# A new column order for the DFT table, and mirror rows stored block by block with plain transfers

## The chip, the cores and the metric

The kernel runs on one core of one Trainium2 chip. The metric is the device time of one execution in microseconds (us). A core has five engines that work side by side, each with an instruction stream of its own: TensorE (PE, with its weight loads shown as PEld), VectorE (DVE), ScalarE (ACT), GpSimd (POOL) and SyncE (SP). SP, ACT and POOL also issue the DMAs; 16 DMA engines carry them.

## The reference

For each of 8 sequences of 3072 tokens with 256 features, the real part of a two-dimensional discrete Fourier transform is taken, and a feed-forward layer with a three-way maximum works on every token:

```
X = np.fft.fft(np.fft.fft(x, axis=1), axis=2).real      # x: (8, 3072, 256)
t = X.reshape(8 * 3072, 256)
h = np.maximum(np.maximum(t @ w1, t @ w2), t @ w3)      # each w: (256, 768)
out = h @ w_out                                         # (768, 256), out: (24576, 256), fp32
```

Inputs and output are fp32. The real input makes token k and its mirror token 3072 - k of a sequence share their work: one is a sum, the other a difference of an even part and an odd part.

## The kernel before

**Stages.** A sequence is first mixed. x is loaded (line 127, POOL's queue, with a cast to bf16) into `xt`; short products with a small table give `tb` (lines 401 to 416); `tb` goes to DRAM as `db` and comes back transposed as `yb` (methods `y` and `z`, lines 419 to 431, SP's queue); then `Mix.k` (line 461) multiplies the 17 column groups of `yb` with the cosine tables `te_tab` and `to_tab`. That gives `tE` and `tO`, the even and the odd part, for 1536 half-tokens of the sequence, in three blocks of 512 columns. The cosine tables are made on the chip from a vector `kvec` of token numbers, by iotas (`ramp`, line 169), a reduction of the angle and sines.

**Column order.** Which token stands in which of the 1536 columns follows from which `yb` group the column is multiplied with. Before, the groups of 96 columns (64 for the last) follow one another: group r holds the tokens r, r + 32, r + 64 and so on. `_parts(g)` (line 39) lists for block g which group covers which columns; each entry is one matmul of `Mix.k` (line 466). A block has 6, 6 and 8 entries.

**The feed-forward layer.** Each block of 512 columns passes six units of 128 hidden features (`begin`, `finish`): `unit_plus` adds even and odd (`hp`, for the tokens), `unit_minus` turns the same sum into the difference (`hm`, for the mirror tokens). For every second unit (`is_split`) the third operand is summed outside PE: DVE makes `even3`, ACT `odd3`, and POOL their sum and difference, `plus` and `minus` (line 828), which DVE's `hp` (line 837) and `hm` (line 849) then need.

**The second layer** (`l2_block`, line 517) runs one block behind, as a generator from which ten steps are taken per unit. A block has four sub-blocks of 128 columns; a slot is a sub-block's number in its sequence, 0 to 11. PE gathers the token half and the mirror half in `po` (line 513), and DVE adds the linear part and writes `ot`, 128 x 512 fp32 (line 541), of which six buffers turn. Then

- the token half goes out on SP's queue in two or three plain stores (line 549). `_runs(slot)` (line 30) lists runs of partitions whose tokens are 32 rows apart in `out`; a row is 1 KB;
- the mirror half goes out on POOL's queue in one indexed store (line 622), emitted by `scatter` at the next unit. Its row numbers stand in `rows_m`, which `rows` (line 697) works out on POOL during the first sequence. Slot 11 stores 127 rows, since its first column is token 0. A one-element memset on `mark` (line 626) follows each.

The last block of the last sequence (`l2_last`, line 552) takes its sub-blocks in the order 3, 0, 1, 2, has the mirror half computed from flipped copies `tEr` and `tOr`, so that its rows ascend too, and issues plain stores from ACT, SP and POOL in turn (line 584). `l2_mid` (line 587) handles token 1536 of all sequences.

**Order.** The order on every engine is written out by hand: `plan` and `ahead` say at which unit of a sequence which piece of the next one's mixing is issued (the yb loads `z0` and `z1` at units 6 and 7), and each engine and queue runs its instructions in that order. DMAs of ACT and SP share eight completion counters in rotation, POOL's another eight.

Of the kernel before, what the change touches and what calls it, by code (L numbers as in the profile page):

```python
# [9 lines left out]
FP32 = mybir.dt.float32  # L10
BF16 = mybir.dt.bfloat16
INT32 = mybir.dt.int32
UINT32 = mybir.dt.uint32
AX = mybir.ActivationFunctionType
ALU = mybir.AluOpType
# [14 lines left out]
def _runs(slot):  # L30

    if slot == 11:
        return [(0, 48, 0), (48, 96, 16), (96, 128, 15 + 32 * 64)]
    t, u = divmod(slot, 3)
    edge, r = 96 - 32 * u, 4 * t + 1 + u
    return [(0, edge, r + 32 * 32 * u), (edge, 128, r + 1)]


def _parts(g):

    cols = [(r, 96 * (r - 1), 96 if r < 15 else 64, 0) for r in range(1, 16)]
    cols += [(0, 1408, 48, 0), (16, 1456, 48, 0), (15, 1504, 32, 64)]
    done = []
    for (r, c, wd, _) in cols:
        a, z = max(c, 512 * g), min(c + wd, 512 * g + 512)
        if a < z:
            done.append(((r - 1) % 16 if r < 16 else 16, a - 512 * g, z - a))
    return done
# [3 lines left out]
def kernel(  # L52
# [9 lines left out]
    nc = tc.nc  # L62

    B, S, D = x.shape
# [50 lines left out]
    rows_m = consts.tile([128, 12 * B], INT32, tag="rows_m")  # L115
    mark = consts.tile([1, 1], FP32, tag="mark")
# [32 lines left out]
    def iota(t, pattern, base=0, cm=0):  # L149
        nc.gpsimd.iota(t, pattern, base=base, channel_multiplier=cm,  # L150
                       allow_small_or_imprecise_dtypes=True)
# [14 lines left out]
    kvec = gen.tile([128, NHALF + 1], FP32, tag="kvec")  # L166
    kv = kvec[:, 0:1440].rearrange("p (r j) -> p r j", j=96)

    def ramp(r):
        n = {0: 6, 6: 5, 11: 4}[r]  # L170
        iota(kv[:, r:r + n, :], [[1, n], [32, 96]], base=r + 1)

    dvec = gen.tile([128, 128], FP32, tag="dvec")
    for c, (s0, s1) in enumerate(FIRST):
        for h in range(2):
            load_x(0, s0, s1, h)
        if c == 0:
            iota(dvec, [[1, 128]])
        elif c < 3:
            ramp((0, 6)[c - 1])  # L180
# [12 lines left out]
    ramp(11)  # L193
    iota(kvec[:, 1408:1504].rearrange("p (r j) -> p r j", r=2), [[16, 2], [32, 48]])
    iota(kvec[:, 1504:NHALF], [[32, 32]], base=15 + 32 * 64)
    iota(kvec[:, NHALF:NHALF + 1], [[0, 1]], base=NHALF)
# [72 lines left out]
    q = gen.tile([128, NHALF + 1], FP32, tag="q")  # L269
# [118 lines left out]
    class Mix:  # L388
# [72 lines left out]
        def k(self, which, g, evict=nc.scalar.copy):  # L461
# [3 lines left out]
            for (i, c0, wd) in _parts(g):  # L465
                nc.tensor.matmul(ps2[:, c0:c0 + wd], self.col(i, which),  # L466
                                 tab[:, g * 512 + c0:g * 512 + c0 + wd], start=True, stop=True)
# [38 lines left out]
    def stored(st, mine, others):  # L506
        for group in others:
            tc.declare_no_dep(st.ins, group=group, reason="each store has rows of its own")
        tc.add_to_no_dep_group(mine, st.ins)
# [7 lines left out]
    def l2_block(b, blk, hp, hm, te, to):  # L517

        base = b * S
        for sub in range(4):  # L520
# [3 lines left out]
            if sub % 2 == 0:  # L524
# [10 lines left out]
            ot = out_pool.tile([128, 512], FP32, name="ot", tag="ot")  # L535
# [6 lines left out]
                out=ot.rearrange("p (h c) -> p h c", h=2),  # L542
                in0=po.rearrange("p (h c) -> p h c", h=2),
                in1=lin.unsqueeze(1).to_broadcast([128, 2, 256]), op=ALU.add)
            lo = 1 if slot == 11 else 0
            waiting.append((b * 12 + slot, lo, ot))
            for (p0, p1, k0) in _runs(slot):
                row = base + k0
                stored(nc.sync.dma_start(out=out[row: row + 32 * (p1 - p0 - 1) + 1: 32, :],
                                         in_=ot[p0:p1, 0:256]), "direct", ("scattered",))  # L550

    def l2_last(hp, hm, te, to, flipped):

        base = (B - 1) * S
        ter, tor = flipped
        for sub in (3, 0, 1, 2):
# [4 lines left out]
            ot = out_pool.tile([128, 512], FP32, name="ot", tag="ot")  # L561
            for (h, tev, tov, wo, hid) in (
                    (0, te[:, cp], to[:, cp], gw[:, 256:512], lambda jc: hp[:, jc, sp]),
                    (1, ter[:, sm], tor[:, sm], gw[:, 512:768], lambda jc: hm[:, jc, sm])):
                if h == 0 or sub == 2:
                    po = ps_o.tile([128, 512], FP32, name="po", tag="po")
# [6 lines left out]
                if sub == 2:  # L573
                    nc.vector.tensor_copy(out=ot[:, h * 256:(h + 1) * 256], in_=ph)
            if sub != 2:
                nc.vector.tensor_copy(out=ot, in_=po)
            stores = [(p0, p1, base + k0, 0) for (p0, p1, k0) in _runs(slot)]
            for (p0, p1, k0) in _runs(slot):
                if k0 == 0:
                    p0, k0 = 1, 32  # L580
                stores.append((128 - p1, 128 - p0, base + S - k0 - 32 * (p1 - p0 - 1), 256))
            for k, (p0, p1, row, c) in enumerate(stores):
                eng = (nc.scalar, nc.sync, nc.gpsimd)[(k + (sub == 2)) % 3]
                stored(eng.dma_start(out=out[row: row + 32 * (p1 - p0 - 1) + 1: 32, :],
                                     in_=ot[p0:p1, c:c + 256]), "direct", ("scattered",))

    def l2_mid():
# [20 lines left out]
        for _ in l2_hidden(po[0:B, 0:256], lambda jc: hmid[:, jc, :]):  # L608
            pass
        ot = out_pool.tile([128, 512], FP32, name="ot", tag="ot")  # L610
        nc.vector.tensor_copy(out=ot[0:B, 0:256], in_=po[0:B, 0:256])
        stored(nc.sync.dma_start(out=out[NHALF: NHALF + S * (B - 1) + 1: S, :],
                                 in_=ot[0:B, 0:256]), "direct", ("scattered",))
# [4 lines left out]
    def scatter():  # L618

        while waiting:  # L620
            at_row, lo, ot = waiting.pop(0)
            stored(nc.gpsimd.indirect_dma_start(  # L622
                out, bass.IndirectOffsetOnAxis(
                    ap=rows_m[0:128 - lo, at_row: at_row + 1], axis=0),
                ot[lo:128, 256:512], None), "scattered", ("scattered", "direct"))
            nc.gpsimd.memset(mark, 0.0)
# [60 lines left out]
    m.c(1, 7)  # L687
# [9 lines left out]
    def rows():  # L697

        rows_f = gen.tile([128, 12 * B], FP32, tag="rows_f")
        iota(rows_f.rearrange("p (b t u) -> p b t u", t=4, u=3), [[S, B], [-4, 4], [-1025, 3]],  # L700
             base=S - 1, cm=-32)
        rows_v = rows_f.rearrange("p (b r) -> p b r", r=12)
        adj = gen.tile([128, 12], FP32, tag="adj")
        adv = adj.rearrange("p (t u) -> p t u", u=3)
        four = pidx.to_broadcast([128, 4])
        pool = nc.gpsimd
        for u in range(3):
            scal(adv[:, :, u], four, float(96 - 32 * u), ALU.is_ge, 3071.0, ALU.mult, eng=pool)
        low = gen.tile([128, 2], FP32, tag="low")
        scal(low[:, 0:1], pidx, 47.0, ALU.is_ge, 1520.0, ALU.mult, eng=pool)  # L710
        scal(low[:, 1:2], pidx, 95.0, ALU.is_ge, -511.0, ALU.mult, eng=pool)
        scal(low[:, 0:1], low[:, 0:1], 2031.0, ALU.add, eng=pool)
        pool.tensor_tensor(out=adj[:, 11:12], in0=low[:, 0:1], in1=low[:, 1:2], op=ALU.add)
        pool.tensor_tensor(out=rows_v, in0=rows_v,
                           in1=adj.unsqueeze(1).to_broadcast([128, B, 12]), op=ALU.add)
        pool.tensor_copy(rows_m, rows_f)

# [5 lines left out]
    out_pool = ctx.enter_context(tc.tile_pool(name="outbuf", bufs=6))  # L723
# [201 lines left out]
```

## Time and profile before

| | us |
|---|---|
| median of 3 runs (394.51 to 395.22) | 394.9 |
| the profiled execution | 395.75 |
| its span, first to last instruction | 393.8 |
| PE busy | 377.7 |
| POOL busy | 332.9 |
| DVE busy | 315.0 |
| ACT busy | 263.0 |

The span lies inside the profiled execution; the difference is what lies around the program's own instructions. Busy time is the time in which an engine has an instruction at work. The granted PE clock was 0.996 of full speed over the span. DMA moved 54.20 MB, 138 GB/s in the mean. A matmul's own duration includes its way through the array, so the pace of a stream of matmuls is read from start to start.

### The profile page before, as it was taken

To read this page: it belongs to the slowest core of one execution; us is meant where nothing else is said; L and a number is where in the kernel's file an instruction comes from. 1 tells how busy PE (TensorE), PEld (TensorE's weight loads), DVE (VectorE), ACT (ScalarE), POOL (GpSimd) and SP (SyncE) were. 2 spreads that over 40 slices of the span, in tenths; PEclk is the share of its full clock that TensorE was granted. 3 is DMA by queue.
4 is the path that set the end of the run, shared out by engine and by line. 5 is a ranking of instruction groups with operands and counts; after the bars stand their busy time and mean duration, and the time that the engine had idled before them with its cause. 6 is when DMAs were issued, how large, how long until landed. Compare 5 with 4: busy or idle time off the path is not lost.

```text
span 393.8 us, 8383 instructions
## 1 busy us (share of the span) xinstructions
PE 377.7 (96%) x2710; PEld 235.9 (60%) x2759; DVE 315.0 (80%) x530; ACT 263.0 (67%) x476; POOL 332.9 (85%) x432
## 2 busy tenths in 40 slices
PE   6698999999999999999999999999999999999994
PEld 2354566566665666565665666556665666666673
DVE  7788897788687788788787888877887887887972
ACT  6877788677766887577867787578866447435420
POOL 8985698979978899889988899889977898869993
PEclk9999999999999999999999999999999999999998
DMA  7999576585838776495767876495333553321234
GB/s 115 159 194 183 131 191 146 114 191 150 161 102 144 190 153 144 117 206 137 137 150 120 210 132 160 118 206 124 108 108 101 131 147 90 94 77 47 90 96 131
DMA packets 66901, 54.20 MB, mean 138 GB/s; under 512 B 32702, under 2 KB 62556, under 8 KB 66003
## 3 DMA queue, kind: packets, MB, share of 16 engines
q0 software_dynamic: 24368, 26.53, 35.5%
q1 hardware_dynamic: 41978, 26.72, 27.0%
q8 instruction: 21, 0.34, 0.4%
q10 hardware_dynamic: 512, 0.43, 0.4%
q14 instruction: 22, 0.18, 0.1%
HBM read 36.95 MB, written 30.81 MB: 172 GB/s over the span
## 4 chain that ended last, share of the span: by engine, by line
PE 84%; DMA 4%; DVE 4%; ACT 3%; issue 2%; POOL 2%; SPq 1%; DVEq 0%; ACTq 0%; POOLq 0%
PE po L513 30%; PE pse L497 12%; PE pse L490 8%; PE pse L491 7%; PE po L536 4%; PE d L821 4%; PE pse L835 4%; PE e L819 3%; PE ps L466 3%; PE pse L836 3%; PE pl L528 2%; PE ps L401 2%; DMA yb<-db 2%; DMA xt<-in_x_dram 2%; ACT tb L405 1%
## 5 line engine op out<-in xcount | busy, mean ns | idle before, releaser
L503 ACT ACTIVATE stmp<-pse 128x512 bf16<-128x512 f32 x150 | 89.6, 600 | 66.1 <-PE pse L497 50.9
L622 POOL DMA_INDIRECT out_dram<-ot,rows_m x92 | 102.4, 1113 | 17.9 <-issue 8.8
L828 POOL TENSOR_TENSOR plus<-even,odd 128x512 bf16<-128x512 f32 x69 | 87.8, 1272 | 32.9 <-DVE even L824 32.7
L828 POOL TENSOR_TENSOR minus<-even,odd 128x512 bf16<-128x512 f32 x69 | 87.5, 1268 | 0.0
L513 PE MATMUL po<-wout_bf,hp 128*128 128x256 bf16 x576 | 86.1, 273 | 0.4
L837 DVE SCALAR_TENSOR_TENSOR hp<-pse,plus 128x512 bf16<-128x512 f32 x69 | 47.6, 689 | 46.5 <-PE pse L836 13.9
L513 PE MATMUL po<-wout_bf,hm 128*128 128x256 bf16 x576 | 78.6, 273 | 0.0
L513 PEld LDWEIGHTS <-hp 128*128 128x128 bf16 x576 | 56.4, 98 | 26.1
L497 PE MATMUL pse<-tO,gd_all 128*128 128x512 bf16 x217 | 70.5, 379 | 1.1 <-DVE hp L504 0.2
L513 PEld LDWEIGHTS <-hm 128*128 128x128 bf16 x576 | 56.4, 98 | 16.3
L541 DVE TENSOR_TENSOR ot<-po,even 128x512 f32<-128x512 f32 x92 | 62.7, 681 | 0.0
L504 DVE TENSOR_TENSOR hp<-pse,stmp 128x512 bf16<-128x512 f32 x75 | 51.4, 685 | 10.1 <-ACT stmp L503 8.7
L490 PE MATMUL pse<-tE,g_all 128*128 128x512 bf16 x148 | 56.0, 379 | 1.9 <-DVE tE L468 0.5
L504 DVE TENSOR_TENSOR hm<-pse,stmp 128x512 bf16<-128x512 f32 x75 | 51.5, 687 | 7.4 <-ACT stmp L503 4.1
L824 DVE SCALAR_TENSOR_TENSOR even<-vb,wcol,e 128x512 f32<-128x512 bf16 x69 | 50.8, 737 | 0.0
L491 PE MATMUL pse<-tO,g_all 128*128 128x512 bf16 x131 | 49.6, 379 | 0.2 <-issue 0.2
L849 DVE SCALAR_TENSOR_TENSOR hm<-pse,minus 128x512 bf16<-128x512 f32 x69 | 47.0, 681 | 0.7
L823 ACT ACTIVATE odd<-d 128x512 f32<-128x512 f32 x69 | 41.3, 598 | 6.2
L134 ACT COPY xt<-xt 64x762 bf16<-64x762 bf16 (+1 forms) x48 | 40.2, 838 | 1.1
L497 PEld LDWEIGHTS <-gd_all 128*128 128x128 bf16 x219 | 21.3, 97 | 22.2 <-issue 4.1
L536 PE MATMUL po<-gw,tO 128*128 128x512 bf16 x85 | 32.3, 380 | 0.0
L405 ACT CAST tb<-ps 128x512 bf16<-128x512 f32 x38 | 20.5, 588 | 14.1 <-PE ps L401 14.1
(175 smaller groups left out, 475.7 us busy)
## 6 DMA issues: line engine op xcount, KB each, us to landing
xt<-in_x_dram POOLq DMA_DIRECT2D x14, 384.0 KB, 8.4
out_dram<-ot SPq DMA_DIRECT2D x55, 96.0 KB
out_dram<-ot SPq DMA_DIRECT2D x64, 64.0 KB
db<-tb SPq DMA_DIRECT2D x21, 192.0 KB
vb<-vd SPq DMA_DIRECT2D x23, 128.0 KB
xt<-in_x_dram POOLq DMA_DIRECT2D x7, 400.0 KB, 6.9
xt<-in_x_dram POOLq DMA_DIRECT2D x7, 368.0 KB, 6.1
out_dram<-ot SPq DMA_DIRECT2D x62, 32.0 KB
```

The lines of the kernel that those rows point to most:

```text
L490: nc.tensor.matmul(pse[:, 0:n], g_all[:, jc, 2 * i, :], te, start=True, stop=False)
L491: nc.tensor.matmul(pse[:, 0:n], g_all[:, jc, 2 * i + 1, :], to, start=False, stop=True)
L497: nc.tensor.matmul(pse, gd_all[:, jc, i, :], to, start=False, stop=True, skip_group_check=True)
L503: nc.scalar.activation(out=stmp[:, 0:n], in_=pses[0][:, 0:n], func=AX.Relu)
L504: nc.vector.tensor_tensor(out=dst, in0=src3, in1=stmp[:, 0:n], op=ALU.max)
L513: nc.tensor.matmul(po, hcols(jc), wout_bf[:, jc * 256:(jc + 1) * 256], start=False, stop=(jc == NJC - 1), skip_group_check=True)
L536: nc.tensor.matmul(po, to[:, cp], gw[:, 256:768], start=True, stop=True)
L541: nc.vector.tensor_tensor(out=ot.rearrange("p (h c) -> p h c", h=2), in0=po.rearrange("p (h c) -> p h c", h=2), in1=lin.unsqueeze(1).to_br ...
L622: stored(nc.gpsimd.indirect_dma_start(out, bass.IndirectOffsetOnAxis(ap=rows_m[0:128 - lo, at_row: at_row + 1], axis=0), ot[lo:128, 256:51 ...
L824: nc.vector.scalar_tensor_tensor(out=even3, in0=vb, scalar=wcol[:, jc:jc + 1], in1=e3, op0=ALU.mult, op1=ALU.add)
L828: nc.gpsimd.tensor_tensor(out=dst, in0=even3, in1=odd3, op=op)
L837: nc.vector.scalar_tensor_tensor(out=dst, in0=pse2, scalar=0.0, in1=sums[g][0], op0=ALU.max, op1=ALU.max)
```

## The change

The columns get another order. In each block of 512, every sub-block of 128 columns holds 96 tokens of one group and 32 tokens of one of the groups 12 to 15, so that partition p of the four sub-blocks holds four neighbouring rows of `out`. `_parts(g)` then has 8, 8 and 9 entries; in block 2 two of them take every second column. `ramp` fills `kvec` in the new order.

A block's output collects in one buffer of 128 x 2048 fp32 (`obufs`, three in turn: one of its own, and the two halves of `kq`, which before are `kvec` and `q`). Sub-block s writes its token half to place s and its mirror half to place 7 - s, so the mirror rows of a partition ascend as well. At the end of a block `stores_plus` lists 4 plain stores for SP (6 for block 2), with 48 or 16 partitions of 4 KB each (3 KB and 1 KB for parts of block 2), and `stores_minus` lists 2 (3 for block 2) for POOL, which `scatter` issues at the next unit. A mirror store covers both halves of 48 or 16 partitions at once, and its rows in `out` go down: the row dimension of the DRAM side has a negative step. `rows`, `rows_m`, `mark`, `_runs` and the indexed stores are gone.

`l2_last` now takes the sub-blocks in the order 1, 2, 3, 0, writes into one of the three buffers, and stores once after sub-block 3 (12 stores) and after each half of sub-block 0 (4 stores each), in turn on ACT, SP and POOL. `m.c(1, 16)` copies fifteen columns at once, where `m.c(1, 7)` and later `m.c(7, 16)` stood.

```
 def _parts(g):
-    cols = [(r, 96 * (r - 1), 96 if r < 15 else 64, 0) for r in range(1, 16)]
-    cols += [(0, 1408, 48, 0), (16, 1456, 48, 0), (15, 1504, 32, 64)]
...
+    done = [(12 + i - 1, slice(128 * i + 96, 128 * i + 128)) for i in range(4)]
+    for i in range(4 if g < 2 else 3):
+        done.append((4 * g + i, slice(128 * i, 128 * i + 96)))
+    if g == 2:
+        done += [(16, slice(384, 480, 2)), (15, slice(385, 480, 2))]
     return done
...
+    def back(v):
+        return v.rearrange("(a j) r d -> a j r d", a=2)[:, ::-1]
+
+    def stores_plus(b, blk, buf, s0=0, s1=4):
+        mine, v = rows_of(b)
+        n = s1 if blk < 2 else min(s1, 3)
+        for a in range(2):
+            j = 48 - 48 * a
+            yield v[j:j + 48, 4 * blk + 1 + s0:4 * blk + 1 + n, :], buf[48 * a:48 * a + 48, s0:n, :]
+            j = 32 * blk + 16 - 16 * a
+            yield v[j:j + 16, 12 + s0:12 + s1, :], buf[96 + 16 * a:112 + 16 * a, s0:s1, :]
+        if n < s1:
+            yield mine[784:784 + 46 * 16 + 1:16, :], buf[0:47, 3, :]
+            yield mine[16:16 + 47 * 16 + 1:16, :], buf[48:96, 3, :]
+
+    def stores_minus(b, blk, buf):
+        mine, v = rows_of(b)
+        n = 4 if blk < 2 else 3
+        r = 32 - 4 * blk
+        yield back(v[0:96, r - n:r, :]), buf[0:96, 8 - n:8, :]
+        yield back(v[64 - 32 * blk:96 - 32 * blk, 17:21, :]), buf[96:128, 4:8, :]
+        if n < 4:
+            yield back(mine[NHALF:S - 15:16, :].unsqueeze(1)), buf[0:96, 4:5, :]
...
     def l2_block(b, blk, hp, hm, te, to):
+        buf = obufs.pop(0)
+        obufs.append(buf)
...
             nc.vector.tensor_tensor(
-                out=ot.rearrange("p (h c) -> p h c", h=2),
-                in0=po.rearrange("p (h c) -> p h c", h=2),
+                out=buf[:, sub:8 - sub:7 - 2 * sub, :], in0=po.rearrange("p (h c) -> p h c", h=2),
                 in1=lin.unsqueeze(1).to_broadcast([128, 2, 256]), op=ALU.add)
-            lo = 1 if slot == 11 else 0
-            waiting.append((b * 12 + slot, lo, ot))
-            for (p0, p1, k0) in _runs(slot):
-                row = base + k0
-                stored(nc.sync.dma_start(out=out[row: row + 32 * (p1 - p0 - 1) + 1: 32, :],
-                                         in_=ot[p0:p1, 0:256]), "direct", ("scattered",))
+        for (dst, src) in stores_plus(b, blk, buf):
+            store(nc.sync, dst, src)
+        waiting.extend(stores_minus(b, blk, buf))
...
     def l2_last(hp, hm, te, to, flipped):
-        for sub in (3, 0, 1, 2):
+        for sub in (1, 2, 3, 0):
...
+                    if sub == 3:
+                        stores = [*stores_plus(B - 1, 2, buf, 1, 4),
+                                  *stores_turned(B - 1, buf, 1, 4)]
+                for k, (dst, src) in enumerate(stores):
+                    store((nc.scalar, nc.sync, nc.gpsimd)[k % 3], dst, src)
...
     def scatter():
         while waiting:
-            at_row, lo, ot = waiting.pop(0)
-            stored(nc.gpsimd.indirect_dma_start(
...
-            nc.gpsimd.memset(mark, 0.0)
+            store(nc.gpsimd, *waiting.pop(0))
```

Here `v` is `out` of one sequence as 96 x 32 rows, `mine` the same as 3072 rows, and `stores_turned` lists the mirror stores of the last block, whose rows ascend.

133 lines of the change are left out of this document (55 added, 78 removed).

## The prediction

> **What bounds the kernel now.** I read the front page first (span, busy time by engine, engine shares of the chain that ended last), then the table of busy time by stretch (its columns: stretch and length, then busy us and instruction count of PE, PEld, DVE, ACT and POOL, the granted clock, the DMA share, GB/s), then the waits and the groups by line, and last short pieces of the timeline (start, duration, engine, line, operation).
>
> ```profile
> span 393.8 us, 8383 instructions
> PE 377.7 (96%) x2710; PEld 235.9 (60%) x2759; DVE 315.0 (80%) x530; ACT 263.0 (67%) x476; POOL 332.9 (85%) x432
> PE 84%; DMA 4%; DVE 4%; ACT 3%; issue 2%; POOL 2%; SPq 1%; DVEq 0%; ACTq 0%; POOLq 0%
> ...
> 46.00:380.00 334.00, 331.27 (x2365) 208.38 (x2410) 273.09 (x428) 228.50 (x406) 289.54 (x348) 1.00 0.59 135
> 380.00:393.80 13.80, 8.42 (x76) 7.15 (x73) 5.49 (x10) 0.48 (x1) 6.51 (x12) 0.89 0.45 126
> ```
>
> PE is the wall: between 46 and 380 us it is busy 331.27 of 334.00 us at the full granted clock (1.00), and it holds 84% of the chain. POOL, which the change relieves, is busy 85% of the span but holds 2% of the chain. So there are only three places where time can move: work added to PE (paid in full), the few PE stalls that exist, and the last 13.8 us, where PE is busy for 8.42 us and the rest is stores.
>
> **Part 1: more pieces in the table product.** The new column order cuts a 512-column block of tE or tO into 8, 8 and 9 matmuls, where it was 6, 6 and 8: 25 for 20 in each of 16 sets (8 sequences, two tables), so 80 more. The columns streamed stay 512. Does a short piece cost only its columns?
>
> ```profile
> 106.09 0.39 PE L466 MATMUL ps<-te_tab,yb 128*128 128x64 bf16 x6
> 106.32 0.38 PE L835 MATMUL pse<-tE,g_all 128*128 128x512 bf16 x1
> 106.54 0.38 PE L836 MATMUL pse<-tO,g_all 128*128 128x512 bf16 x1
> ...
> 108.71 0.41 PE L466 MATMUL ps<-to_tab,yb 128*128 128x32 bf16 x8
> 108.97 0.38 PE L497 MATMUL pse<-tO,gd_all 128*128 128x512 bf16 x1
> ...
> 68.08 0.16 PE L481 MATMUL ps<-te_tab,yb 128*128 128x1 bf16 x1
> 68.10 0.16 PE L481 MATMUL ps<-to_tab,yb 128*128 128x1 bf16 x1
> ```
>
> From start to start, one 512-column matmul takes 0.22 us (106.32 to 106.54), so a column takes 0.42 ns. Six pieces of 96 and 64 take 0.23 (106.09 to 106.32); eight pieces, two of them of 32 columns, take 0.26 (108.71 to 108.97). One-column matmuls still start 0.02 apart, so there is a floor per matmul. 32 columns at 0.42 ns would be 0.013, below the floor; the extra 0.03 or 0.04 of the eight-piece group, shared by its two 32s, its two 48s and the joins, puts a 32-column piece at about 0.026, a 48 or 64 at 0.028 and a 96 at 0.042 (at 0.42 ns a column 64 and 96 would be 0.027 and 0.040). Then a new block 0 or 1 is 4 x 0.042 + 4 x 0.026 = 0.27 and block 2 is 4 x 0.026 + 3 x 0.042 + 2 x 0.028 = 0.286, against 0.236, 0.224 and 0.263 before: 0.107 more per set, 16 x 0.107 = **+1.7 us**, all of it on the path. The two 48-column pieces read and write every second column, which no row shows; if that halves their pace it is 16 x 2 x 0.02 = 0.6 more. Below nothing is excluded, since no columns go. Bounds 0 to +2.3.
>
> The page "TensorE: Matmul & The Clock Gate" of the Trainium skill (section "Back-to-back issue gap") speaks against short pieces: it puts a sustained weight-load and matmul pair at about 81 ns for 128 columns. By that the 80 pieces would be 6.5 us and the sum 4.8 us longer; the trace disagrees, with 0.23 us for six such pairs.
>
> **Part 2: POOL's indexed stores go.** 92 indexed stores and their 92 small memsets go; 53 plain stores come, two or three together at each block's end, and six of the tail's twenty. The groups by line, the counts of line 622 and its landing times (issue to landed), and the timeline:
>
> ```profile
> L622 POOL DMA_INDIRECT out_dram<-ot,rows_m x92 | 102.4, 1113 | 17.9 <-issue 8.8 <-DVE hm L504 5.6 <-DVE hp L837 1.9
> L626 POOL MEMSET mark<- 1x1 f32 x92 | 8.1, 88 | 0.2
> L584 POOL DMA_DIRECT2D out_dram<-ot x5 | 2.7, 535 | 1.7 <-DVE ot L576 1.6
> ...
> L622 POOL DMA_INDIRECT out_dram<-ot,rows_m x92: 960/986/2553, 47.5 to 383.5; - x92
> DMA to landing us min/median/max: 2.4/3.5/12.8
> ...
> 134.04 2.55 POOL L622 DMA_INDIRECT out_dram<-ot,rows_m  x1 [0.22 <-DVE hm L504]
> 136.63 1.28 POOL L828 TENSOR_TENSOR plus<-even,odd 128x512 bf16<-128x512 f32 x1
> 137.95 0.69 DVE L837 SCALAR_TENSOR_TENSOR hp<-pse,plus 128x512 bf16<-128x512 f32 x1 [1.64 <-PE pl L528]
> ```
>
> A plain store of 32 to 96 rows takes 0.54 us. I allow up to 0.8 for the new ones, which are larger: still cheaper than 1.11 + 0.09, so POOL sheds some 110 us and gets back at most 59 x 0.8 = 47. PE sees that only where POOL makes it wait, and there is one such place in a sequence: the store of slot 11, with 127 rows, takes 2.55 us, the `plus` behind it is late, and DVE idles 1.64 us until it can do `hp` at 137.95, right when `plus` ends. The wait then reaches PE:
>
> ```profile
> 94.08 0.82 PE L513 MATMUL po<-wout_bf,hm 128*128 128x256 bf16 x6
> 94.86 0.39 PE L536 MATMUL po<-gw,tO 128*128 128x512 bf16 x1
> 95.08 0.38 PE L513 MATMUL po<-wout_bf,hp 128*128 128x256 bf16 x2
> 95.45 0.38 PE L835 MATMUL pse<-tE,g_all 128*128 128x512 bf16 x1
> ...
> PEld L536 <- DVE ot L541: 1.7, 7, 0.2
> ```
>
> Six 256-column matmuls at 0.109 (256 x 0.42 ns) are 0.655, but the next starts 0.78 later; two are 0.218, but the next starts 0.37 later: 0.28 us lost, 7 times. In the new program POOL has three plain stores at this place (1.6 to 2.4) where it had a median store, the slow one and their memsets, 0.99 + 2.55 + 2 x 0.09 = 3.7. `plus` comes over 1 us earlier, the stall needs 0.3, so it goes: 7 x 0.28 = **-2.0 us** (bounds 0, if the plain stores take 1.2 each, to -2.0). What is late next is PE itself.
>
> **Part 3: SP's queue.** SP's stores move from every sub-block to the end of a block, 4 or 6 of them with rows of 3 or 4 KB. Behind block 2's six stand the four yb loads of the next sequence, which before stood two and two around a store that waits for DVE. Once this cost PE time, in the second steady sequence:
>
> ```profile
> 89.82 1.50 SPq L549
> 91.80 7.90 DMA yb<-db
> ...
> ACT yb L455 <- DMA yb<-db: 1.4, 1, 1.4
> L584 SPq DMA_DIRECT2D out_dram<-ot x6: 315/370/547, 383.9 to 389.5; - x6
> ...
> 99.40 0.82 PE L513 MATMUL po<-wout_bf,hp 128*128 128x256 bf16 x6
> 103.92 0.38 PE L497 MATMUL pse<-tO,gd_all 128*128 128x512 bf16 x1
> 145.09 0.82 PE L513 MATMUL po<-wout_bf,hp 128*128 128x256 bf16 x6
> 148.83 0.38 PE L497 MATMUL pse<-tO,gd_all 128*128 128x512 bf16 x1
> ```
>
> The same piece of the program takes 4.52 us here and 3.74 in the next sequence: 0.78 lost while ACT waits for a load issued at 91.80. In the new order that load follows the six stores directly, at 0.37 us an issue, and is spared the 1.50 us for which SP stood at the store of 89.82, and that store's wait for DVE; ACT lacked 1.4: **-0.8 us** (bounds -0.8, and +0.8 for each of the six other sequences if the loads now come late, a rival below).
>
> **Part 4: the tail.** The last block now does sub-blocks 1, 2, 3, then 0; twelve stores go out together after sub-block 3, four after each half of sub-block 0, in turn on ACT, SP and POOL. The old tail in the timeline, the landing times of its stores (line 584), and its one wait of SP for a DMA:
>
> ```profile
> 386.64 0.69 DVE L576 COPY ot<-po 128x512 f32<-128x512 f32 x1 [1.05 <-PE po L513]
> 388.92 0.47 SPq L584 DMA_DIRECT2D out_dram<-ot  x1
> 389.49 0.55 SPq L584 DMA_DIRECT2D out_dram<-ot  x1
> DMA to landing us min/median/max: 2.9/3.7/4.6
> SPq L584 <- DMA out_dram<-ot: 1.2, 1, 1.2
> ```
>
> Now SP's last store is issued at 389.49 and the program ends 4.3 us later. Even here one store waited 1.2 us for an older one to land: a queue may not issue a store while the one eight places back, on the same counter, is in flight. In the built order of the changed program SP's second store after sub-block 3 has 47 rows, and SP's first store of sub-block 0 shares its counter. The 47-row store of the old tail was issued first, with 5 us to land; the new one goes at 386.64 + 0.69 + 0.37 = 387.7. With the longest landing of this group, 4.6, it lands at 392.3; the store that waited for it goes then and the last one 0.4 later, at 392.7, where it was 389.49: +3.2. With the shortest, 2.9, it is +1.5. I take the long end, since 47 does not split evenly and the slow store of part 2 (127 rows, 12.8 us at most) is of the same kind, less 0.3 because the final landing meets less traffic: **+2.9 us**.
>
> **At nothing.** The iotas of the ramps are two more (0 to +0.2, by the 88 ns of POOL's smallest instruction above), beside x loads in flight. `rows` (small POOL operations of the first sequence) goes, with no wait of PE on it in the list of waits; `c(1,16)` is one ACT copy for two. The three 8 KB buffers are reused three blocks, one sequence, later: 148.83 - 103.92 = 44.9 us, far beyond 12.8 us of landing, so DVE does not wait.
>
> **Sum:** +1.7 - 2.0 - 0.8 + 2.9 = +1.8 us on the span: 393.8 to 395.6. The profiled execution took 395.75 us, 1.95 more than its span and 0.85 over the median of 394.9; on the median the forecast is 396.7. Its own range, from the bounds: 395.2 (tail +1.5, all else as taken) to 398.1 (strided pieces +0.6, half of part 2 kept, tail +3.3).
>
> **Rivals.** *Two engines for a mirror store.* POOL's new stores write DRAM as 2 x 48 or 2 x 16 rows from 96 or 32 partitions. If such a shape is served by few DMA engines, as the 127-row store seems to be (12.8 us against 3.5), the last big one, 393 KB, ends late. The first queue moves 26.72 MB in 27.0% of 16 engines' span:
>
> ```profile
> q1 hardware_dynamic: 41978, 26.72, 27.0%
> 381.29 0.68 DVE L541 TENSOR_TENSOR ot<-po,even 128x512 f32<-128x512 f32 x1
> ```
>
> That is 15.7 GB/s an engine, 12.5 us for 393 KB on two. Issued at 382 and with 2.4 us at least, it lands at 396.9, and shares its engines with the tail. That is some 2.3 us past the forecast's tail: 399. The page "DMA: Bandwidth & Descriptors" of the Trainium skill (section on why a DMA increments its semaphore by 16) says that the engine count divides the outermost size of both sides, which is 2 here, though it names exceptions on POOL's path. For it: the slow 127-row store. Against: nothing here shows this shape. *Late yb loads.* Bursts of 1 MB at a block's end slow the loads behind them; if all seven sequences then lose 0.78, it is 396.7 + 0.8 + 4.7 = 402. Against it: six of seven now have no wait. *Faster.* The tail's wait does not bind, because the 47-row store lands within 3 us while other stores are still being issued; then parts 1 to 3 stand alone, -1.1 us: 393.8. It decides as soon as part 4 costs under 0.3.
>
> **Chances.** Forecast 0.52, two engines 0.25, late loads 0.10, faster 0.13. A measurement here can tell about 0.2%, 0.8 us, from no change. Range 394.6 to 400.5: it takes in the forecast, the two-engine case and the near part of the late loads. Faster by over 0.2% (below 394.1): 0.12; within: 0.13, the forecast's low end and the faster case's high end; slower (over 395.7): 0.75.
>
> **What would show it.** Right: 400 table matmuls with PE busy about 1.7 us more; POOL busy near 265 us; no PE gap of 0.13 and 0.15 us once a sequence; yb no longer ending an ACT wait; a gap of some 3 us before SP's last stores, where now the last one goes at 389.49. Wrong: PE gaps in mid-kernel after block 2, plain POOL stores over 1 us, stores landing after 10 us, or a tail no longer than before.

## The result

The changed kernel takes 447.47 us (median of 4 runs, 443.0 to 448.79) against 394.99 (394.51 to 395.22): ratio 1.131, 95% interval 1.123 to 1.139. The forecast was 396.7 with a range to 400.5. The profiled execution took 446.86 us, its span is 445.1.

From the page and the views of the changed kernel (busy time and instruction count of each engine; PE's busy share and granted clock in 40 slices; packets; DMA queue; shares of the chain that ended last; two groups of mirror stores, with the size of one and the median us to landing; the landing times of all GpSimd's stores):

```profile
span 445.1 us, 8136 instructions
PE 386.6 (87%) x2790; PEld 241.3 (54%) x2839; DVE 318.4 (72%) x530; ACT 262.4 (59%) x475; POOL 256.0 (58%) x294
PE   6799999993999849997599965999589999999990
PEclk9999999996999969999699996999979999999997
DMA packets 72244, 54.23 MB, mean 122 GB/s; under 512 B 46718, under 2 KB 64901, under 8 KB 71348
q0 software_dynamic: 39680, 26.67, 33.2%
PE 67%; DMA 22%; DVE 3%; POOL 2%; issue 2%; ACT 2%; SPq 0%; POOLq 0%; DVEq 0%; ACTq 0%
out_dram<-obuf POOLq DMA_DIRECT2D x8, 384.0 KB, 12.6
out_dram<-kq POOLq DMA_DIRECT2D x8, 384.0 KB, 11.4
DMA to landing us min/median/max: 7.7/11.3/19.1
```

PE, whose slices were all full in mid-kernel, now has five holes (slices 10, 14 and 15, 19 and 20, 24 and 25, 29 and 30), and the granted clock dips in or just behind them. DMAs hold 22% of the chain that ended last, where they held 4%. GpSimd's stores land in a median of 11.3 us after their issue. The list of waits (us in total, times, longest) names what PE stands for; the last row is the kernel before:

```profile
ACT yb L447 <- DMA yb<-db: 44.7, 5, 9.9
PE ps L458 <- ACT yb L448: 37.3, 5, 8.4
DVE hp L844 <- POOL plus L835: 1.5, 1, 1.5
DVE hp L837 <- POOL plus L828: 8.6, 7, 1.7
```

DVE, which waited seven times for `plus` behind the slow store of part 2, now waits once. The first hole on the chain (start, length, what):

```profile
83.85 4.90 DMA db<-tb
88.76 0.75 DVE even L831
89.52 8.24 DMA out_dram<-kq
97.78 9.67 DMA yb<-db
107.54 0.07 ACT yb L447
107.83 0.21 PE ps L458
```

SyncE issues the last of the four yb loads only at 97.78, since a store issued at 89.52, eight places back on the same counter, is in flight for 8.24 us. The load then takes 9.67 us. How much of this is new shows beside a run of the next section, the one with the positive step, whose mirror stores aren't slow. SyncE's queue at this place (start, length, line, operation, count), the changed kernel first:

```profile
80.93 5.73 SPq L415 DMA_DIRECT2D db<-tb  x2
86.76 8.96 SPq L499 DMA_DIRECT2D out_dram<-kq  x6
95.81 2.25 SPq L421 DMA_DIRECT2D yb<-db  x4
```

```profile
80.56 1.28 SPq L415 DMA_DIRECT2D db<-tb  x2
82.39 4.83 SPq L499 DMA_DIRECT2D out_dram<-kq  x6
87.32 1.50 SPq L421 DMA_DIRECT2D yb<-db  x4
```

There the last load goes out at 88.36, 9.42 us earlier. By the landings in its trace the store that is in flight for 8.24 us here takes 1.97, but the load takes 9.25, hardly less than the 9.67 here. So in the first hole nearly all of the loss is the late issue. The third hole is the exception: its last load takes 13.21 us (9.02 in that run), in the other four 8.6 to 9.9 (8.6 to 9.3). The first and the last of the five holes, then the stretch behind each of the five (stretch and length, busy us and count of PE, PEld, DVE, ACT and POOL, granted clock, DMA share, GB/s):

```profile
100.30:107.80 7.50, 0.25 (x3) 0.00 (x0) 0.00 (x0) 0.26 (x3) 2.96 (x4) 0.75 1.03 215
318.10:323.90 5.80, 0.01 (x1) 0.01 (x1) 0.00 (x0) 0.29 (x3) 1.97 (x3) 0.88 0.60 172
107.80:120.00 12.20, 12.07 (x106) 7.90 (x109) 8.88 (x14) 8.99 (x16) 4.62 (x4) 0.88 0.28 72
162.10:182.00 19.90, 19.74 (x157) 12.53 (x160) 15.18 (x24) 13.18 (x24) 9.30 (x9) 0.92 0.30 77
216.70:236.00 19.30, 19.14 (x153) 12.36 (x156) 14.58 (x23) 13.18 (x24) 8.88 (x9) 0.91 0.25 67
271.70:291.00 19.30, 19.14 (x153) 12.30 (x156) 14.76 (x23) 13.19 (x24) 9.05 (x9) 0.92 0.27 70
323.90:336.00 12.10, 11.99 (x91) 7.45 (x94) 7.95 (x12) 8.74 (x16) 3.45 (x3) 0.78 0.26 49
```

In the first hole the DMA engines are full (1.03) while PE, VectorE and ScalarE all but stand. About half of the packets' time there belongs to the x loads on GpSimd's queue, and 2% to the data of mirror stores. The last hole comes long after the last x load (issued at 293.9), with a DMA share of 0.60, so full engines aren't needed for a hole. Behind a hole PE is busy but at a lower clock. As an estimate, the missing share of the clock times the stretch is 1.5 to 1.7 us for each of the first four holes (0.12 of 12.2 us, and so on) and 2.7 for the last.

### The profile page after: what moved, and what is told of

It is laid out like the page before. It is cut to its first block, busy times and chain, and to the rows that moved or that the text cites. A ratio compares the mean times of both kernels' runs of the same rounds, so it can differ in the third digit from the quotient of the medians.

```text
span 445.1 us, 8136 instructions
## 1 busy us (share of the span) xinstructions
PE 386.6 (87%) x2790; PEld 241.3 (54%) x2839; DVE 318.4 (72%) x530; ACT 262.4 (59%) x475; POOL 256.0 (58%) x294
## 2 busy tenths in 40 slices
DMA packets 72244, 54.23 MB, mean 122 GB/s; under 512 B 46718, under 2 KB 64901, under 8 KB 71348
## 4 chain that ended last, share of the span: by engine, by line
PE 67%; DMA 22%; DVE 3%; POOL 2%; issue 2%; ACT 2%; SPq 0%; POOLq 0%; DVEq 0%; ACTq 0%
PE po L553 22%; DMA yb<-db 11%; PE pse L489 10%; DMA out_dram<-kq 8%; PE pse L483 5%; PE pse L482 5%; PE po L576 3%; PE ps L458 3%; PE pse L842 3%; PE d L828 3%; PE e L826 3%; PE pse L843 3%; PE ps L393 2%; PE pl L569 2%; DMA xt<-in_x_dram 1%
## 5 line engine op out<-in xcount | busy, mean ns | idle before, releaser
L553 PE MATMUL po<-wout_bf,hm 128*128 128x256 bf16 x576 | 79.7, 275 | 0.3
L489 PE MATMUL pse<-tO,gd_all 128*128 128x512 bf16 x218 | 73.0, 391 | 0.6
L482 PE MATMUL pse<-tE,g_all 128*128 128x512 bf16 x137 | 51.9, 379 | 1.5 <-DVE tE L460 0.4
L458 PE MATMUL ps<-to_tab,yb 128*128 128x32 bf16 (+2 forms) x200 | 11.7, 200 | 37.3 <-ACT yb L448 37.3
L581 DVE TENSOR_TENSOR kq<-po,even 128x512 f32<-128x512 f32 x60 | 41.0, 683 | 0.1
L458 PEld LDWEIGHTS <-yb 128*128 128x128 bf16 x400 | 18.2, 99 | 41.2 <-ACT yb L448 38.7
L576 PE MATMUL po<-gw,tO 128*128 128x512 bf16 x92 | 35.1, 382 | 0.0
```

The source lines that it names most:

```text
L458: nc.tensor.matmul(ps2[:, cols], self.col(i, which), tab[:, g * 512:(g + 1) * 512][:, cols], start=True, stop=True)
L482: nc.tensor.matmul(pse[:, 0:n], g_all[:, jc, 2 * i, :], te, start=True, stop=False)
L489: nc.tensor.matmul(pse, gd_all[:, jc, i, :], to, start=False, stop=True, skip_group_check=True)
L553: nc.tensor.matmul(po, hcols(jc), wout_bf[:, jc * 256:(jc + 1) * 256], start=False, stop=(jc == NJC - 1), skip_group_check=True)
L576: nc.tensor.matmul(po, to[:, cp], gw[:, 256:768], start=True, stop=True)
```

## The experiments

All ratios below are to the kernel before, run on the same chip in the same series.

**Is it the negative step, or the outermost size 2?** The theory: each mirror store has 2 as its outermost size in DRAM and its data is carried by two DMA engines. The rivals: the negative step is slow in itself, or any 1 MB burst is. First the step alone was turned round:

```
     def back(v):
-        return v.rearrange("(a j) r d -> a j r d", a=2)[:, ::-1]
+        return v.rearrange("(a j) r d -> a j r d", a=2)
```

> The changed kernel with one edit: the mirror stores keep their shape (2 x 48 and 2 x 16 rows in DRAM, from 96 and 32 partitions), but the inner step is positive, so the rows within each half land in ascending order and not in mirrored order. Two engines: the shape alone decides, so nothing changes: 440 to 455 us, GpSimd's stores land in a median of 11 us as before this edit, PE's wait for yb stays near 37 us. Negative step: if the descending addresses are what is slow, the stores land in 3 to 5 us and the time falls to 393 to 399. Bursts (1 MB of stores at each block's end delay what stands behind them, whatever their shape): 440 to 455.

Measured: 396.64 us, ratio 1.0045 (1.0029 to 1.006). That looks like the answer "negative step", and it is not one. With an ascending step the second half follows the first at the same distance (48 x 8192 = 393216 elements), and the built program has one dimension of 96 rows in place of 2 x 48: the edit took away two things at once. The expectation had overlooked that.

The second run cut each of these stores into its halves (`for a in range(2): yield v[48 * a:48 * a + 48, ...], buf[48 * a:48 * a + 48, ...]`):

> As the run with the positive step, but each mirror store is cut into its two halves, 48 or 16 rows from 48 or 16 partitions: the same bytes, rows, packets and moments, twice the stores on GpSimd's queue. Two engines: the outermost size is now 48 or 16, all engines share a store, it lands in 3 to 6 us, PE's wait for yb falls from 37 us to under 3, the clock is back at 0.99 or more, and the time is 393 to 399. Bursts: the bytes come at the same moments, so the time stays at 430 to 455. Negative step is not tested by this run alone: it gives 393 to 399 too, but then the run before it does as well.

Measured: 397.88 us, ratio 1.0077 (1.0064 to 1.0091). Bursts are out: the same bytes at the same moments cost nothing like 50 us. It tells shape from step no better than the run before it, and is 1.2 us slower than that, with 53 more stores on GpSimd.

Two further runs change one thing each. Outermost 2 with a positive step that can't be merged:

```
-        return v.rearrange("(a j) r d -> a j r d", a=2)[:, ::-1]
+        return v.rearrange("(j a) r d -> a j r d", a=2)
```

> The changed kernel with one edit: the inner step of the mirror stores is positive, and the two halves write every second place (DRAM [8192, 2], [16384, 48], [1, 1024] in elements), so that the two outer dimensions can't be merged into one of 96, as they could in the run with the positive step; the rows land in another order. Outermost size 2 decides: 440 to 455 us again, GpSimd's stores land in some 11 us, and the packets under 512 B are 46,700 as in the changed kernel. Negative step decides: 396 to 398 us, and under 28,500 packets below 512 B.

and a negative step under an outermost size of 48 or 16:

```
-        return v.rearrange("(a j) r d -> a j r d", a=2)[:, ::-1]
+        return v.rearrange("(j a) r d -> j a r d", a=2)[:, ::-1]
```

> The changed kernel with the dimensions of the mirror stores the other way round: the inner step is still negative, but over 2 rows, and the outermost size is 48 or 16 (DRAM [16384, 48], [-8192, 2], [1, 1024]); the rows land in another order. Outermost size decides: 396 to 398 us, and under 28,500 packets below 512 B. Negative step decides: 440 to 455 us, and 46,700 such packets.

Measured: 446.76 us, ratio 1.130 (1.1272 to 1.1328), and 396.54 us, ratio 1.0039 (1.0024 to 1.0053). The packets and the landing times of GpSimd's stores (min/median/max), first with outermost 2 and a positive step, then with outermost 48 and a negative one:

```profile
DMA packets 72243, 54.23 MB, mean 122 GB/s; under 512 B 46717, under 2 KB 64900, under 8 KB 71347
DMA to landing us min/median/max: 7.7/11.1/14.3
PE ps L458 <- ACT yb L448: 38.1, 5, 9.2
```

```profile
DMA packets 52867, 54.13 MB, mean 137 GB/s; under 512 B 27285, under 2 KB 45468, under 8 KB 51971
DMA to landing us min/median/max: 3.1/4.7/9.3
```

That settles it: the outermost size decides, the sign of the step does not. The trace doesn't tell the engines apart, but its packets fit a count of them. The changed kernel has 46,718 - 27,285 = 19,433 more packets under 512 B than the last run; the list of packets has them as packets of 4, 8 and 16 bytes on GpSimd's queue. If 14 of 16 engines carry no data but one 4-byte piece for each of the 48 (or 16) rows of an engine that does, 16 stores of 2 x 48 rows of 4 KB give 16 x 14 x 48 and 23 of 2 x 16 rows give 23 x 14 x 16, together 15,904 packets of 4 bytes; the list of packets has 17,584 against 1,680 of that size, just 15,904 more. (The rest, 2,352 of 8 bytes and 1,176 of 16, are block 2's: 7 x 14 x 48 = 4,704 pieces each, two or four in a packet.)

The kernel before holds the same sign. Its packets of 16 and 12 bytes, 3,255 and 105 on GpSimd's queue, make 13,335 pieces of 4 bytes, just 7 x 15 x 127: that fits one engine for each of its seven slow stores of 127 rows. In the run below that cuts this store into 64 and 63 rows, 49 and 49 such packets make 343 pieces, 7 x 7 x 7: nine engines for 63 rows, and no idle one for 64.

The Trainium skill, page "DMA: Bandwidth & Descriptors", section "Why a DMA increments its semaphore by 16 and not by 1", has the rule: the number of engines is the largest up to 16 that divides the outermost sizes of both sides. It holds here, on GpSimd's queue too: by these packets 2 for 2 x 48, 1 for 127, 9 for 63, and 16 for 48 x 2, for 96 and for 32, where no such pieces are added.

**How do slow stores stop PE?** Keeping the mirror stores as they are, SyncE's six stores of block 2 went behind the yb loads:

```
-        for (dst, src) in stores_plus(b, blk, buf):
-            store(nc.sync, dst, src)
+        mine = list(stores_plus(b, blk, buf))
+        if blk == 2 and b < B - 2:
+            late.extend(mine)
+            mine = []
+        for (dst, src) in mine:
+            store(nc.sync, dst, src)
...
             mm.z(int(what[1]))
+            while what[1] == "1" and late:
+                store(nc.sync, *late.pop(0))
```

> The changed kernel with its mirror stores as they are; SyncE's six stores of block 2 are issued behind the four yb loads of the next sequence, not ahead of them (six of seven sequences have these loads ahead in the steady part). If the loss comes because the loads are issued late (SyncE stands at a store whose counter is taken by a store in flight, 8.2 us in the chain), the loads go out 6 to 8 us earlier, PE's wait for yb falls from 37 us to under 10 and the time to 400 to 415. If the loads are late because their DMA engines are busy with the mirror stores' bytes whenever they are issued, they land at the same moment as now: wait over 25 us, time over 430.

Measured: 418.77 us, ratio 1.0613 (1.0591 to 1.0634). The waits of this run:

```profile
ACT yb L447 <- DMA yb<-db: 14.0, 3, 7.3
PE ps L458 <- ACT yb L448: 12.1, 4, 5.8
```

and the chain at its longest hole:

```profile
235.99 0.51 SPq L421
236.55 11.55 DMA yb<-db
248.48 0.61 PE ps L458 x8
```

It lies between the two expectations. Taking the stores away from in front of the loads saves 25 of PE's 37 us. In the 12 that remain no output store stands before the loads. Two things are left: SyncE stands 24.0 us, in seven waits, for the write of `db` that the loads read (1.7 us in one wait in the run with the positive step), and the load itself takes 11.55 us in this hole, where the loads of that run took at most 9.3. How much each of the two costs, no run separates.

**Without the shape.** The mirror rows by indexed stores again, but of 3 or 4 rows in a run for each of 128 partitions, four stores a sequence; all else as in the changed kernel:

```
-        yield back(v[0:96, r - n:r, :]), buf[0:96, 8 - n:8, :]
-        yield back(v[64 - 32 * blk:96 - 32 * blk, 17:21, :]), buf[96:128, 4:8, :]
+        at = 4 * b + blk
+        yield rows_m[:, at:at + 1], buf[:, 8 - n:8, :].rearrange("p f c -> p (f c)")
         if n < 4:
-            yield back(mine[NHALF:S - 15:16, :].unsqueeze(1)), buf[0:96, 4:5, :]
+            yield rows_m[:, at + 1:at + 2], buf[:, 4, :]
```

> The changed kernel with the new column order and the stores of SyncE as they are, but the mirror rows go by indexed stores again, now with 3 or 4 rows in one run for each of 128 partitions: four indexed stores a sequence where the kernel before has twelve. Two engines: with one address for each partition a store is spread over all engines again, as in the kernel before (median landing 3.5 us there); 393 to 398 us, GpSimd busy about 20 us less than in the changed kernel. Bursts: still 1 MB at a block's end, 430 to 455.

Measured: 396.28 us, ratio 1.0032 (1.002 to 1.0044); GpSimd was busy 259.0 us, not less than the changed kernel's 256.0: this part of the expectation was wrong, since 30 long indexed stores at 1.0 us take about what 53 plain ones took.

**Part 1 alone.** The kernel before, its pieces cut to 8, 8 and 9:

```
         a, z = max(c, 512 * g), min(c + wd, 512 * g + 512)
+        while z - a == 64 or 0 < z - a and a in (0, 32):
+            done.append(((r - 1) % 16 if r < 16 else 16, a - 512 * g, 32))
+            a += 32
```

> The kernel before with part 1 alone: its column order and its stores stay, but the pieces of the table product are cut to 8, 8 and 9 per block with the widths of the changed kernel (32, 32, 32, 32 and four 96; and so on), side by side, not strided. Part 1 as priced: 80 more matmuls, +1.7 us, 396.6 us, PE busy 1.7 us more. If a short piece cost 81 ns, as a rule of the Trainium skill has it for 128 columns (page TensorE: Matmul & The Clock Gate, Back-to-back issue gap), +6.5 us. If joins cost nothing, 395.

Measured: 396.49 us against 395.02, ratio 1.0043 (1.0029 to 1.0057): +1.1 to +2.3 us, forecast +1.7. Here the pieces of block 2 lie side by side. In the run with the positive step, where two of them take every second column, block 2's two groups take 0.298 and 0.342 us from start to start, against 0.282 and 0.308 here (the second with a one-column matmul at its end in both): the strides cost 0.05 us a sequence, 0.4 us in all.

**Part 2 alone.** The kernel before with `lo = 16 if slot == 11 else 0`:

> The kernel before with part 2 alone: the indexed store of slot 11 takes 112 rows, not 127 (15 mirror rows of each of seven sequences are not written, the others of this sub-block go to other rows); everything else is as it was. Part 2 as priced: the store takes 1.0 us instead of 2.55, the wait of 1.64 us before hp goes, and PE gains 0.28 us seven times: -2.0 us, 393.0 us. If PE's 0.13 and 0.15 us have another cause: no change, 394.9. The landing of this store falls from 12.8 to some 3.5 us as well, which would show in SyncE's yb load of the second steady sequence (a further -0.8 at most).

Measured: 395.02 us against 395.02, ratio 1.0003 (0.9989 to 1.0017). No change, yet the mechanism is there. The same matmul in two sequences that follow one another (start, duration, engine, line), in part 1 alone (with a second matmul some 5 us ahead of it), in part 2 alone, and in the run with the long indexed stores:

```profile
98.01 0.38 PE L500 MATMUL pse<-tO,gd_all 128*128 128x512 bf16 x1
103.37 0.38 PE L500 MATMUL pse<-tO,gd_all 128*128 128x512 bf16 x1
143.11 0.38 PE L500 MATMUL pse<-tO,gd_all 128*128 128x512 bf16 x1
148.47 0.38 PE L500 MATMUL pse<-tO,gd_all 128*128 128x512 bf16 x1
```

```profile
102.35 0.38 PE L497 MATMUL pse<-tO,gd_all 128*128 128x512 bf16 x1
146.91 0.38 PE L497 MATMUL pse<-tO,gd_all 128*128 128x512 bf16 x1
```

```profile
103.16 0.38 PE L491 MATMUL pse<-tO,gd_all 128*128 128x512 bf16 x1
147.98 0.38 PE L491 MATMUL pse<-tO,gd_all 128*128 128x512 bf16 x1
```

A sequence takes 45.10 (103.37 to 148.47), 44.56 and 44.82 us, where the kernel before took 44.91 (103.92 to 148.83 in the prediction's rows): part 1 costs 0.19 a sequence, part 2 saves 0.35, both together save 0.09, and 0.05 of the missing 0.07 is the strides. In each of these runs the steady sequences agree within 0.1 us. What part 2 saves is lost at the very end, in the last instruction of GpSimd's queue (count, min/median/max ns, first and last start), first of the kernel before, then of part 2 alone:

```profile
L920 POOLq DRAIN  x3: 46/103/4820, 388.2 to 393.5; - x3
```

```profile
L920 POOLq DRAIN  x3: 46/103/7678, 384.5 to 392.7; - x3
```

The long DRAIN stands from 388.21 to 393.03 before and from 384.52 to 392.2 here, while SyncE is through at 391.95 and at 388.2. GpSimd's last store had landed at 390.89 and 386.97. So the DRAIN ends 2.1 us after the last landing in one kernel and 5.2 in the other, with the same stores in the tail. PE ended 3.7 us earlier (384.73 against 388.42), the span only 0.8.

**The tail.** To the run with the long indexed stores, one edit: the store of 47 rows in two.

```
-            yield mine[784:784 + 46 * 16 + 1:16, :], buf[0:47, 3, :]
+            for (p0, p1) in ((0, 32), (32, 47)):
+                yield mine[784 + 16 * p0:784 + 16 * p1 - 15:16, :], buf[p0:p1, 3, :]
```

> The run with the long indexed stores (396.28 us) with one edit: the store of 47 rows is cut into 32 and 15, in the tail and at each block 2. Part 4 as told: SyncE's second store after sub-block 3 (issued 386.31, landed 390.21 there) holds the queue until 390.27 and the last store until 391.24; cut, both halves land in some 2 us, SyncE's last store goes out by 389.5 and its last wait ends 1.5 to 2 us earlier: 394.3 to 395.0. The counters' rotation moves by one with the added store, so another store may be stood for (1 us): then 395.3. If GpSimd's DRAIN at the end (393.53 there, 0.5 us after SyncE's last) sets the end by itself: 395.8.

Measured: 395.43 us against 395.14, ratio 1.0009 (1.0 to 1.0018); the run it builds on had 1.0032 (1.002 to 1.0044). SyncE's stand for stores in flight, before and after the cut:

```profile
SPq L503 <- DMA out_dram<-kq: 3.3, 2, 2.7
```

```profile
SPq L503 <- DMA out_dram<-kq: 1.5, 3, 0.8
```

Two more edits of the tail: the 48-partition stores of sub-blocks 1 and 2 already after sub-block 2 (`tail_early`, called when `sub == 2`), and then the last eight stores on ScalarE and SyncE alone (the others then take turns beginning with GpSimd).

> The run with 47 cut, and in the tail the four stores of sub-blocks 1 and 2 (48 x 2 rows each) go out after sub-block 2, 1.7 us earlier; nine stores, not thirteen, then wait for sub-block 3. If the tail is bound by issues and by landings on shared counters: another 0.5 to 1 us off, 393.5 to 394.3, faster than the kernel before by 0.2 to 0.35%. If GpSimd's DRAIN sets the end: within 0.3 of the run before it.

> As the run before it, but the eight stores of the last sub-block go to ScalarE and SyncE alone, and GpSimd's last store is one of sub-block 3, about 1.5 us earlier. If GpSimd's DRAIN follows its last store by a fixed 4.3 us and sets the end: 1 us off, 393 to 393.5. If the counters that ScalarE and SyncE share are the bound: 0.5 to 1.5 us longer than the run before it. In the run with the short store of slot 11 that DRAIN ended 7.1 us after GpSimd's last store was issued, with the same stores as before in the tail, so what it waits for is not known.

Measured: 395.11 us, ratio 0.9994 (0.9985 to 1.0003), and 394.50, ratio 0.9984 (0.9972 to 0.9997). The first gained 0.3 where 0.5 to 1 was expected; the second gained 0.6 more. Each step alone is within the intervals; the two together, from 1.0009 to 0.9984, are just beyond them. In the second the DRAIN ended at 391.31 and SyncE was the last, at 391.68.

**The kernel before, mended.** The slow store of slot 11 cut into 64 and 63 rows, and no tail store on GpSimd:

```
+            if lo:
+                waiting.append((rows_m[0:64, b * 12 + slot: b * 12 + slot + 1], ot[1:65, 256:512]))
+                waiting.append((rows_x[0:63, b:b + 1], ot[65:128, 256:512]))
...
-                eng = (nc.scalar, nc.sync, nc.gpsimd)[(k + (sub == 2)) % 3]
+                eng = (nc.scalar, nc.sync)[(k + (sub == 2)) % 2]
```

> The kernel before with two edits, all rows written: the indexed store of slot 11 (127 rows) is cut into 64 and 63 (the index column of the second moved to partition 0), and in the tail the stores go to ScalarE and SyncE in turn, none to GpSimd. In the run with the short store of slot 11 PE ended 3.7 us earlier and the span only 0.8, since GpSimd's DRAIN ended 5.2 us after its last store had landed (2.1 in the kernel before). If that DRAIN follows GpSimd's last DMA, whatever it waits for, it now ends by 389, ScalarE and SyncE set the end, and the time falls with PE: 391.5 to 392.5 us, 0.6 to 0.9% faster than before. If the DRAIN ends where it did in any case (392.2): 394.5 to 395. If the cut store costs GpSimd as much as the slow one (2 x 1.0 us and two memsets, against 2.55 and one), PE gains nothing and the time is 394.5 to 395.5.

Measured: 392.35 us against 395.22, ratio 0.9931 (0.9918 to 0.9944), the fastest here. Its span is 390.6; the DRAIN now ends at 388.54, again 5.4 us after GpSimd's last landing (383.18), but that is before SyncE is through at 389.87. The two edits were made at once, so their shares aren't told apart by the time. A sequence takes 44.56 us, as with the short store.

## Why the prediction was wrong, and where it was right

**The step that failed is part 3, SyncE's queue.** It let SyncE's six stores of block 2 go out "at 0.37 us an issue", with the yb load right behind them, and took 0.8 us off; what GpSimd's new stores do to SyncE's was put at nothing. The runs show the cost there: the six stores took 8.96 us to go out (4.83 in the run with the positive step, 2.02 for the last five), the last load left 9.42 us later than in that run, and PE stood 37.3 us for yb. The cause was on the list, as the rival "two engines for a mirror store", with a chance of 0.25. It was the right mechanism, but its term was mis-sized: 2.3 us, in the tail alone, where it cost 50.2 us (span 445.1 against 394.9 in the run whose halves merge, the same program otherwise). Two of the prediction's own signs of being wrong came: PE gaps in mid-kernel, and stores that land after 10 us. The last DVE copy of the two, the changed kernel first:

```profile
434.23 0.42 DVE L610 COPY kq<-po 128x256 f32<-128x256 f32 x1 [0.52 <-PE po L553]
```

```profile
387.10 0.43 DVE L610 COPY kq<-po 128x256 f32<-128x256 f32 x1 [0.52 <-PE po L553]
```

So 47.1 us are lost ahead of the tail and 3.1 in it. Of the 47.1, PE's waits for yb are 37.3, the lower clock behind the five holes some 9 by the estimate above, and under 1 is not assigned.

The prediction had most numbers for this. It put such a store at 12.5 us, two or three of them leave at each block's end, and the yb load stands there too: in the one row that showed its margin (issued at 91.80, 7.90 us, ACT lacking 1.4) it had none. In the run with the positive step it has little: the load of the first hole lands at 97.61 there and ACT takes it at 98.44. A load with so small a margin passes nearly all of a delay on to PE, once a sequence; instead the delay was looked for only where the stores themselves end. Why a store on all engines is held up by one on two (8.24 us in flight against 1.97) is not shown, since the trace doesn't name the engine of a packet. That the two busy engines are shared is the likely reason; what the added small packets cost by themselves no run separates.

**The rival "late yb loads"** (0.10, 402 us) was listed as a case of its own, with 0.78 us a sequence. It was the other one's consequence, through the issue more than through the transfer, and a hole was 5.8 to 8.4 us. Two rivals that can be cause and effect of one another should be worked out as one chain.

**Part 1** was right: forecast 0.21 us a sequence, measured 0.19 in the steady part, and 1.47 us (1.1 to 2.3) in the whole against 1.7. The strided pieces, allowed 0.6, cost 0.4 in all. The 81 ns for 128 columns of the Trainium skill (page "TensorE: Matmul & The Clock Gate", section "Back-to-back issue gap") gave 6.5 us; this run disagrees, with 1.1 to 2.3 for the 80 pieces.

**Part 2** was right in its mechanism and somewhat small: 0.35 us a sequence against 0.28. That it alone brings no time at all was not foreseen: in its profile GpSimd's DRAIN takes it back.

**Part 3** also counted a loss twice. In the run with part 1 alone, whose stores and loads stand in the old order, the stretch in question takes 5.36 us in both sequences (98.01 to 103.37, 143.11 to 148.47), and in its trace ACT stands before a yb load only in two later sequences, 0.8 us in all (put down to another DMA), with the sequences still at 45.1 to 45.2 us. So the loss probably belonged to the one execution that was profiled, 395.75 us against a median of 394.9; a second profile of the kernel before would show it. The prediction took 0.85 us off for that difference, and 0.8 more for its cause.

**Part 4** was right in size: from the last DVE copy to the end the kernel before takes 5.4 us (388.46 to 393.8), the run whose halves merge 7.8, the long indexed stores 7.3; forecast was 2.9 more, measured 2.4 and 1.9. The 47-row store is less of it than was thought: cut, it gives back 0.9 us (1.0032 to 1.0009). The two edits behind it gave back 0.9 more; that the rest is the number of stores that leave together, and the DRAIN, is likely but not shown.

**The sum.** Where the mirror stores are carried by all engines, the change does what the likeliest case said: 396.28, 396.54 and 396.64 us in three forms, forecast 396.7; the fourth, in halves with 53 more stores, takes 397.88. Part of that agreement is luck, since 0.8 us of part 3 and 0.5 to 1 us of part 4 cancel. The upper end of the forecast's own range was also added up wrongly: +0.6, +1.0 and +0.4 on 396.7 are 398.7, not 398.1. "At nothing" held for the iotas, `rows` and the buffers: none of them is in the list of waits on PE's path.

## What to carry to other kernels

Before a store is made of more dimensions, look at the outermost size of both sides in the program as built: a reversed half turns 96 rows into 2 x 48, and the transfer from 16 engines to 2. When one transfer gets slower, follow it to every queue that shares its engines or counters, and ask there which load has little margin. Compare the load's own time with a run without the slow transfer before you call the load slow: here it was issued late. And an edit that takes away a suspect can take away a second one with it (the sign and, by merging, the shape), so read the built form of each experiment before its verdict.

## What the runs showed of the hardware

- A store whose data lies on few engines adds small packets: as many 4-byte pieces as the idle engines (14 of 16) times the rows of a busy one, some 19,400 packets over the run. They let the number of engines be read from a trace.
- A slow store on GpSimd's queue holds up SyncE's: the store that was in flight for 1.97 us took 8.24.
- GpSimd's DRAIN at the program's end can be the last thing to finish. From the last landing of GpSimd's stores to its end it took 0.95 us (changed kernel, loads first, interleaved), 1.4 (long indexed stores, in all four kernels with them), 1.9 (positive step, and negative pairs), 2.1 (before, and part 1 alone), 3.2 (halves), 5.2 and 5.4 (slot 11 shortened, and cut). It is alike in kernels with the same GpSimd stores, so it is hardly an accident of a run; what it waits for stays open. In the last experiment, with no tail store on GpSimd, it ended before SyncE.
- A hole of 7 to 8 us in PE's stream costs, by estimate, some 1.6 us more behind it, through the granted clock (0.88 over the next 12 us). Behind the hole of 5.8 us it was 2.7 (0.78 over 12 us).
